# The last 64 queries of two head pairs as one attention unit on all 128 rows

## The chip, the cores and the metric

The kernel runs on one core of a Trainium2 chip. The metric is the device time of one execution in microseconds (us); a kernel's time is the median of its runs. TensorE (PE) multiplies, VectorE (DVE), ScalarE (ACT) and GpSimd (POOL) work on vectors, and SyncE (SP) issues most transfers (DMA). Each engine takes its instructions in the order in which they stand in its own queue, and waits in place if one isn't ready.

## The reference

Attention over a window of 128 positions with a bias that falls with the distance, and then a feed-forward layer with a GELU written with a sigmoid:

```python
# q, k, v: (B=8, H=8, S=576, D=64)
scores = 1/sqrt(D) * q @ k.T                 # per batch and head
scores = where(0 <= rel < 128, scores - slope[h] * abs(rel), -1e9)   # rel = query - key position
attn = exp(scores - max(scores)); attn = attn / (sum(attn) + 1e-9)
x = (attn @ v) as (B*S = 4608 tokens, H*D = 512)
h = x @ w_in                                 # 512 -> 2048
out = (h / (1 + exp(-1.702 * h))) @ w_out    # 2048 -> 512
```

Everything is float32 in and out.

## The kernel before

**Attention units.** Attention is cut into units, each a class instance that later steps hang their tiles on. For batches 2 to 7 a unit is made by `whole_batch`, and the change doesn't touch it. For batches 0 and 1 (`WB = 2`) a batch is cut into three ranges of queries, 0 to 256, 256 to 512 and 512 to 576, and `part_batch` makes one `WholeUnit` for each of the four head pairs (`hp`) in each range. So a batch has 12 units: four with 256 queries, four more with 256, and four with the last 64, called tail units here. A `WholeUnit` holds both heads of its pair (`hh` 0 and 1): q and k lie with the 64 features of head 0 on partitions 0 to 63 and those of head 1 on 64 to 127. Its queries are cut into blocks of up to 128 rows; a tail unit has one block of 64 rows, with 192 keys (the 128 before the range and its own 64).

The steps of such a unit, with the tiles that the profile names:

- `load_whole`, `load_whole_v`: q into `rq`, k into `rk`, v into `VV`.
- `scores`: a float32 product for each block and head, head 0 into `s_ps` and head 1 into `sb_ps` (two PSUM tiles; outside the first four units `sb_ps` is one of the two buffers of `t_ps`).
- `biased` (DVE): scores plus the bias table, into `pb`, and the row's extreme into `mins`.
- `exponents` (ACT): the exponential of `pb`, its sums into `totals`.
- `normal`: DVE makes `rec`, the reciprocals of the sums; POOL scales head 0's block, ACT head 1's.
- `flip_whole`: PE transposes the weights, 128 keys at a time, into `t_ps`; ACT (head 0) and DVE (head 1) copy them to `pw`.
- `mix_whole`: PE multiplies `VV` with `pw` into `x_ps`, head 0 into partitions 0 to 63, head 1 into 64 to 127; ACT copies the result into `xf`, the feed-forward's input.

**Ticks.** A tick advances the units as a pipeline: in tick n unit n is scored and its v is loaded, unit n-1 goes through `biased`, `exponents` and `normal`, unit n-2 is flipped, unit n-3 is mixed, and q and k of unit n+4 are loaded. So the number of units is the number of ticks. Seven ticks run before the feed-forward begins.

**Feed-forward.** Chunks of 256 tokens (`T`), 16 steps (`f`) each: `up` is 12 products into `h_ps`, then a tanh and a product on ACT and DVE (`g`, `gh`), a remainder on POOL (`gl`); `down` is 6 products into `acc`. The first steps go with `decode`, which unpacks a weight block (`rw` into `wc`, `bits`, `w`) on ACT, DVE and POOL, 32 times; its `bits` sits in one of the two PSUM buffers of `h_ps`. The first chunk's first 8 steps come first, then chunk 1, then chunk 0's other 8, then chunks 2 to 11. The last six chunks are taken in pairs by another scheme (`accs`, `X_ps`, `Y_ps`).

**What sets the order.** `advance` places ticks between the steps. For each range it holds a due entry: so many units by the step at which a chunk begins, and it spreads the ticks that are left evenly over the steps that are left. In the program thus written each engine's queue is then put in order by a list scheduler when the kernel is built, apart from transfers that `move` keeps in the order of the program.

## Time and profile before

| | |
|---|---|
| runs | 1047.8, 1050.3, 1045.43 us (median 1047.8) |
| the profiled execution | 1047.39 us, of which the span of instructions is 1045.6 us |
| granted TensorE clock | 0.996 of full speed over the span |
| PE busy | 1027.1 us (98%) |
| ACT, DVE, POOL busy | 675.8, 651.1, 621.2 us (65%, 62%, 59%) |
| DMA | 151.91 MB, mean 145 GB/s |

A row of the timeline gives the start, the length, the engine, the line, the operation with the tiles, the form and how many instructions; in brackets stands the idle time ahead and what ended it. `64*64 64x192` means that a part of the PE array with 64 rows and 64 columns was used, with 192 columns streamed from 64 partitions. A float32 product shows as two instructions, a transposition as one. PE's instructions overlap, so what one costs is the distance from its start to the next start, and not its length.

### The profile page before, as it was taken

Reading aid. Unit: us, or ns where it says so; the run is one execution under the profiler, and the core shown is the slowest. Engines: PE = TensorE matmul, PEld = TensorE weight load, DVE = VectorE, ACT = ScalarE, POOL = GpSimd, SP = SyncE. Lnnn points to the kernel's source line nnn. Section 1 sums busy time; section 2 is a strip of 40 time slices with the busy share of each in tenths; the row PEclk is TensorE's granted clock in tenths of the full one; section 3 lists DMA queues with packets and bytes.
Section 4 is the critical chain, followed back from the end, with each engine's and each line's share of the span. In section 5 each row is a group of like instructions: output and inputs, shape, how many; then the busy total and the mean of one; then the engine's idle time right before and its main releaser. Section 6 shows DMA issues by size and latency. Waiting matters only on the chain.

```text
span 1045.6 us, 21874 instructions
## 1 busy us (share of the span) xinstructions
PE 1027.1 (98%) x6897; PEld 906.8 (87%) x6897; DVE 651.1 (62%) x2250; ACT 675.8 (65%) x1978; POOL 621.2 (59%) x858
## 2 busy tenths in 40 slices
PE   8899999999999999999999999999999999999998
PEld 5577778789999999999999999999898998998997
DVE  6786756367777677777777676766743445346343
ACT  6888855478787777877777786877633334335332
POOL 3687866568677677768667686766542224224221
PEclk9899999999999999999999999999999999999999
DMA  8995445423333233334323433432175556456551
GB/s 290 365 354 167 152 134 159 130 77 100 97 110 100 77 90 121 108 100 129 95 80 102 130 108 90 128 104 68 57 276 181 174 172 219 162 181 207 179 180 61
DMA packets 120275, 151.91 MB, mean 145 GB/s; under 512 B 40032, under 2 KB 96864, under 8 KB 120160
## 3 DMA queue, kind: packets, MB, share of 16 engines
q1 hardware_dynamic: 114400, 140.55, 43.2%
q10 hardware_dynamic: 5760, 9.96, 2.7%
q8 instruction: 55, 0.90, 0.4%
q14 instruction: 60, 0.49, 0.1%
HBM read 119.01 MB, written 31.46 MB: 144 GB/s over the span
## 4 chain that ended last, share of the span: by engine, by line
PE 89%; DMA 4%; DVE 3%; ACT 2%; issue 1%; POOL 1%; SPq 0%; POOLq 0%; ACTq 0%; DVEq 0%
PE h_ps L579 24%; PE acc L599 24%; PE accs L779 12%; PE X_ps L720 6%; PE s_ps L352 5%; PE x_ps L518 5%; PE Y_ps L720 4%; PE t_ps L461 4%; PE x_ps L495 2%; PE t_ps L438 1%; PE sb_ps L342 1%; DMA x<-xf 1%; PE s_ps L342 1%; DMA VV<-v 1%; DMA rk<-k 1%
## 5 line engine op out<-in xcount | busy, mean ns | idle before, releaser
L579 PE MATMUL h_ps<-xh,w 128*128 128x256 f32 x1536 | 245.7, 285 | 2.3 <-DVE g L585 1.4
L579 PEld LDWEIGHTS h_ps<-xh,w 128*128 128x128 f32 x1536 | 212.5, 189 | 18.5 <-DVE g L585 3.3
L599 PE MATMUL acc<-w,gh 128*128 128x512 f32 x768 | 216.3, 399 | 0.8 <-ACT half L616 0.4
L589 POOL TENSOR_TENSOR gl<-g,gh 128x256 fp32r<-128x256 f32 x192 | 144.7, 755 | 100.1 <-ACT gh L588 79.9
L732 POOL TENSOR_TENSOR gs<-g,gs 128x512 fp32r<-128x512 f32 x48 | 63.4, 1320 | 169.9 <-PE Y_ps L720 120.5
L599 PEld LDWEIGHTS acc<-w,gh 128*128 128x128 f32 x768 | 131.2, 188 | 21.3 <-ACT half L616 1.2
L779 PE MATMUL accs<-w,gs 128*128 128x512 f32 x576 | 148.3, 393 | 0.3 <-POOL gs L732 0.3
L579 PE MATMUL h_ps<-xl,w 128*128 128x256 f32 x768 | 138.2, 283 | 0.0
L330 POOL TENSOR_TENSOR K<-rk,K 128x384 fp32r<-128x384 f32 (+1 forms) x120 | 108.6, 905 | 43.0 <-ACT K L328 34.7
L599 PE MATMUL acc<-w,gl 128*128 128x512 f32 x384 | 125.7, 405 | 0.0
L585 DVE SCALAR_TENSOR_TENSOR g<-g,h_ps 128x256 f32<-128x256 f32 x192 | 80.0, 417 | 65.0 <-ACT g L584 62.9
L584 ACT ACTIVATE g<-h_ps 128x256 f32<-128x256 f32 x192 | 72.9, 381 | 70.4 <-PE h_ps L579 61.0
L779 PEld LDWEIGHTS accs<-w,gs 128*128 128x128 f32 x576 | 102.3, 189 | 17.6 <-POOL gs L732 0.7
L579 PEld LDWEIGHTS h_ps<-xl,w 128*128 128x128 f32 x768 | 112.0, 189 | 5.8 <-issue 1.5
L399 ACT ACTIVATE pb<-pb,mins 128x256 f32<-128x256 f32 (+2 forms) x216 | 104.7, 486 | 9.1 <-DVE mins L380 8.6
L588 ACT CAST gh<-g 128x256 fp32r<-128x256 f32 x192 | 77.6, 405 | 41.7 <-DVE g L585 33.4
L380 DVE CUSTOM_DVE_ANT_0 pb<-s_ps,bias 128x256 f32<-128x256 f32 (+3 forms) x240 | 86.1, 380 | 26.5 <-PE s_ps L352 23.4
L424 DVE TENSOR_SCALAR_CACHE_REDUCE pb<-pb,rec 128x256 f32<-128x256 f32 (+2 forms) x216 | 91.1, 454 | 2.9
L329 POOL TENSOR_TENSOR Q<-rq,Q 64x256 fp32r<-64x256 f32 (+1 forms) x120 | 81.8, 682 | 11.7 <-ACT Q L310 2.3
L480 DVE TENSOR_TENSOR pl<-t_ps,ph 128x512 fp32r<-128x512 f32 (+2 forms) x120 | 72.9, 607 | 16.7 <-ACT ph L474 15.6
L461 PE MATMUL t_ps<-ident,pb 128*128 128x128 f32 x408 | 76.7, 272 | 0.0
L352 PE MATMUL s_ps<-K,Q 128*128 128x256 f32 (+1 forms) x432 | 75.8, 288 | 0.0
(114 smaller groups left out, 2000.9 us busy)
## 6 DMA issues: line engine op xcount, KB each, us to landing
ring<-part SPq DMA_DIRECT2D x84, 512.0 KB, 3.3
rk<-kT SPq DMA_DIRECT2D x72, 192.0 KB, 2.8
rq<-qT SPq DMA_DIRECT2D x96, 128.0 KB, 2.6
out<-o ACTq DMA_DIRECT2D x34, 256.0 KB, 2.9
rw<-w_in SPq DMA_DIRECT2D x16, 512.0 KB, 6.7
rw<-w_out SPq DMA_DIRECT2D x16, 512.0 KB, 7.2
x<-xf SPq DMA_DIRECT2D x13, 512.0 KB, 3.5
xf<-x SPq DMA_DIRECT2D x13, 512.0 KB, 4.3
```

The source lines that it names most:

```text
L329: nc.gpsimd.tensor_tensor(Q[D:], rq[D:], Q[D:].bitcast(F32), ALU.subtract)
L330: nc.gpsimd.tensor_tensor(K2, rk, K1.bitcast(F32), ALU.subtract)
L352: nc.tensor.matmul(u.s[:b.rows, e, b.first:b.end], u.Q[:, b.q0 - u.q0:b.q0 - u.q0 + b.rows], k[:, ko:ko + b.end - b.first], start=(z == 0) ...
L380: nc.vector.tensor_tensor_reduce(b.p[ra:rb, cs:b.end], u.s[ra:rb, e, cs:b.end], bias[head][ra:rb, cs:b.end], -SCALE, BIG, ALU.add, ALU.min ...
L399: nc.scalar.activation(live, live, AF.Exp, bias=u.mins[:b.rows, e:e + 1], scale=-1.0, accum_out=u.sums[:b.rows, e, :1],)
L424: nc.vector.tensor_scalar(live, live, u.rec[:rows, e:e + 1], None, ALU.mult, ALU.add, u.rec[:rows, 2 + e:3 + e])
L461: nc.tensor.transpose(u.t[:c.n, w:w + b.rows], b.p[:b.rows, col:col + c.n], ident[:b.rows, :b.rows])
L579: nc.tensor.matmul(h, w1[f][:, z, k * P:(k + 1) * P], x[:, k], start=(n == 0), stop=(n == len(ops) - 1))
L589: nc.gpsimd.tensor_tensor(gl, g, gh.bitcast(F32), ALU.subtract)
L599: products.append(nc.tensor.matmul(acc, g[:, t * P:(t + 1) * P], w2[f][:, z], start=(f == self.f0 and n == 0), stop=(f == self.f1 - 1 and ...
L720: nc.tensor.matmul(bank, w[:, z, k * P:(k + 1) * P], x[:, y, k], start=start and i == 0, stop=i == len(ops) - 1, skip_group_check=True)
L779: products.append(nc.tensor.matmul(self.acc[t], g[:, y, t * P:(t + 1) * P], w2[f][:, z], start=(f == 0 and n == 0), stop=(f == NF - 1 and ...
```

## The change

For batches 0 and 1 the four tail units of a batch become two. A `TailUnit` holds two neighbouring head pairs (`pairs = 2`): the 64 queries of the first pair stand on rows 0 to 63 and those of the second on rows 64 to 127 of the same tiles. q and k of both come with one transfer each, into tiles viewed as `[partition, pair, n]`; v takes one transfer for both pairs' first 128 keys and one for each pair's last 64, of which the second lands in a tile of its own (`rv`). There are four score products as before, each on a quarter of the array, and four calls on DVE (64 rows each), since the bias differs by head. The exponentials, the reciprocals, the scaling, the transpositions and the copies are done once for both pairs on 128 rows. The mixing takes eight products of 64 columns, and one copy brings both pairs into `xf`.

```diff
+class TailUnit(WholeUnit):
+    pairs = 2
+
 def part_batch(b, lo, hi):
+    if hi - lo == HALF:
+        return [TailUnit(b, hp, lo, hi) for hp in range(0, NP, 2)]
     return [WholeUnit(b, hp, lo, hi) for hp in range(NP)]
...
+        if u.pairs == 2:
+            both = slice(u.pair, u.pair + 2)
+            u.rq = u.rq[:, :P].rearrange("p (a n) -> p a n", a=2)
+            u.rk = u.rk.rearrange("p (a n) -> p a n", a=2)
+            move(u.rq, q0[both, :, u.lo:u.hi].rearrange("a p n -> p a n"))
+            move(u.rk, k0[both, :, u.k0:u.hi].rearrange("a p n -> p a n"))
+            return
...
+        if u.pairs == 2:
+            last = raw.tile([P, 3, D], F32, name="rv", bufs=2)
+            u.ends = u.rv[:HALF, 2], last[:HALF, :2]
+            move(u.rv[:, :2], v0[u.pair:u.pair + 2, u.k0:end].rearrange("a p h d -> p a h d"))
+            for a in range(2):
+                move(u.ends[a], v0[u.pair + a, end:u.hi])
+            return
...
+            if u.pairs == 2:
+                for a in range(2):
+                    for hh in range(2):
+                        r = slice(hh * D, (hh + 1) * D)
+                        products.append(nc.tensor.matmul(
+                            u.s[hh][a * HALF:(a + 1) * HALF, 0, :P + HALF], u.rq[r, a], u.rk[r, a],
+                            start=True, stop=True))
+                in_turn(products)
+                return
...
+            if u.pairs == 2:
+                for hh in range(2):
...
+                    for a in range(2):
+                        r, n = slice(a * HALF, (a + 1) * HALF), P + HALF
+                        nc.vector.tensor_tensor_reduce(
+                            p[r, :n], u.s[hh][r, 0, :n], bias[2 * (u.hp + a) + hh][r, a * HALF:a * HALF + n],
+                            -SCALE, BIG, ALU.add, ALU.min, u.mins[r, hh:hh + 1],
+                        )
+                    u.p.append((p, p[:, :n], hh))
+                return
...
-            rows, ne = u.blocks[0][1], len(u.p)
+            rows, ne = u.blocks[0][1] * u.pairs, len(u.p)
...
-                    p, rows = u.p[2 * i + hh][0], u.blocks[i][1]
+                    p, rows = u.p[2 * i + hh][0], u.blocks[i][1] * u.pairs
...
+                if u.pairs == 2:
+                    for k in range(2):
+                        ks = slice(k * HALF, (k + 1) * HALF)
+                        products.append(nc.tensor.matmul(
+                            x[hh * D:(hh + 1) * D, ks], u.ends[k][:, hh] if c else u.rv[:, k, hh], p[:, ks],
+                            start=c == 0 and k == 0, stop=c == 1, skip_group_check=True,
+                        ))
+                    continue
...
+        if u.pairs == 2:
+            ct, o = divmod(u.b * S + u.lo, T)
+            nc.scalar.copy(
+                home(ct)[:, u.hp:u.hp + 2, o:o + n], x[:, :2 * n].rearrange("p (a n) -> p a n", a=2))
+            return
```

There are now 92 units instead of 96, and so four ticks fewer. In batch 0 the tail units were units 8 to 11 and are now 8 and 9; in batch 1 they were 20 to 23 and are now 18 and 19. By the pacing rule the ticks 7 to 10 stand at steps 1 to 4 in both kernels; ticks 11, 12, 13, 14 and 15 move from steps 7, 10, 13, 16 and 19 to steps 8, 12, 16, 20 and 24; from step 65 on the two kernels' ticks coincide, four numbers apart.

On PE, at the end of step 0 of the feed-forward, the order was this (`s_ps` and `sb_ps` with 64x192 are tail units' scores, first of unit 8 and then of unit 9; `t_ps` are transpositions of the units ahead of them; `h_ps` is step 1):

```order
L342 MATMUL s_ps<-rk,rq 64x192
L438 MATMUL t_ps<-ident,pb 128x128 x8
L342 MATMUL sb_ps<-rk,rq 64x192
L438 MATMUL t_ps<-ident,pb 128x128 x4
L342 MATMUL s_ps<-rk,rq 64x192
L438 MATMUL t_ps<-ident,pb 128x128 x4
L579 MATMUL h_ps<-xh,w_1_554 128x256 x8
L579 MATMUL h_ps<-xl,w_1_554 128x256 x4
L342 MATMUL sb_ps<-rk,rq 64x192
```

And now, at the same place (line 365 holds the scores of a tail unit, 484 the transpositions):

```order
L365 MATMUL s_ps<-rk,rq 64x192
L484 MATMUL t_ps<-ident,pb 128x128 x8
L365 MATMUL sb_ps<-rk,rq 64x192
L365 MATMUL s_ps<-rk,rq 64x192
L365 MATMUL sb_ps<-rk,rq 64x192
L484 MATMUL t_ps<-ident,pb 128x128 x6
L365 MATMUL s_ps<-rk,rq 64x192
L484 MATMUL t_ps<-ident,pb 128x128 x2
L638 MATMUL h_ps<-xh,w_1_554 128x256 x8
L638 MATMUL h_ps<-xl,w_1_554 128x256 x4
L365 MATMUL sb_ps<-rk,rq 64x192
L365 MATMUL s_ps<-rk,rq 64x192
```

Three of a unit's four score products now stand together behind the first, and unit 9's first one still stands ahead of step 1.

On DVE, in the same stretch, the order was this (`ISA pb,mins` is the bias step on a head's scores, `wc` and `bits` are two steps of the decoding, `COPY pw` frees a transposition's PSUM):

```order
L369 ISA pb,mins<-sb_ps,bias_78 64x192
L369 ISA mins 64x1
L229 SCALAR_TENSOR_TENSOR wc<-wc,bits 128x512
L228 TENSOR_SCALAR bits<-rw_3_288 128x512
L410 TENSOR_REDUCE rec<-totals 64x2
L411 RECIPROCAL rec<-rec 64x2
L369 ISA pb,mins<-s_ps,bias_79 64x192
L369 ISA mins 64x1
L229 SCALAR_TENSOR_TENSOR wc<-wc,bits 128x512
L228 TENSOR_SCALAR bits<-rw_3_290 128x512
L446 COPY pw<-t_ps 128x512
L229 SCALAR_TENSOR_TENSOR wc<-wc,bits 128x512
```

And now, from the same decoding step (`bits<-rw_3_288`) on:

```order
L237 TENSOR_SCALAR bits<-rw_3_288 128x512
L456 TENSOR_REDUCE rec<-totals 128x2
L457 RECIPROCAL rec<-rec 128x2
L238 SCALAR_TENSOR_TENSOR wc<-wc,bits 128x512
L237 TENSOR_SCALAR bits<-rw_3_290 128x512
L492 COPY pw<-t_ps 128x512
L238 SCALAR_TENSOR_TENSOR wc<-wc,bits 128x512
L237 TENSOR_SCALAR bits<-rw_4_347 128x512
L238 SCALAR_TENSOR_TENSOR wc<-wc,bits 128x512
L237 TENSOR_SCALAR bits<-rw_4_349 128x512
L401 ISA pb,mins<-s_ps,bias_81 64x192
L401 ISA mins 64x1
```

Unit 9's first bias step stood between two decoding steps, ahead of three `wc`; now it stands behind them.

On SP's queue of transfers, behind the loads of unit 9, the order was this (tail units 10 and 11, weights 7 and 11 and the v of unit 8):

```order
L166 DMA rq<-q 128x64
L166 DMA rk<-k 128x192
L166 DMA rw_7_545<-w_in 128x512
L166 DMA rw_7_547<-w_out 128x512
L166 DMA rq<-q 128x64
L166 DMA rk<-k 128x192
L166 DMA rw_11_766<-w_in 128x512
L166 DMA rw_11_768<-w_out 128x512
L166 DMA VV<-v 128x128
```

And now, at the same place:

```order
L175 DMA rq<-q 128x256
L175 DMA rk<-k 128x256
L175 DMA rw_7_545<-w_in 128x512
L175 DMA rw_7_547<-w_out 128x512
L175 DMA rq<-q 128x256
L175 DMA rk<-k 128x256
L175 DMA rw_11_766<-w_in 128x512
L175 DMA rw_11_768<-w_out 128x512
L175 DMA VV<-v 128x2x128
```

Units 10 and 11 are now the first two of batch 1, with 256 queries and 256 keys, so that their larger loads take the places of the two tail units' loads.

More of the change, by code (lines that the diff above doesn't have):

```diff
@@ L134 @@
     whole = True
+    pairs = 1
     def __init__(self, b, hp, lo, hi):
@@ L360, in biased @@
             u.p = []
+            if u.pairs == 2:
+                for hh in range(2):
+                    if hh:
+                        p = att.tile([P, 3 * P], F32, name="pb", tag="K1")
+                    else:
+                        p = att.tile([P, 2 * P], F32, name="pb", bufs=5)
+                    for a in range(2):
[6 more added lines that the diff above has]
+                return
             for i, (at, rows) in enumerate(u.blocks):
```

## The prediction

> **What bounds the kernel now.** I read the busy times by stretch first, since the change lies in the first third of the span. The columns are length, then PE, PE's weight loads, DVE, ACT, POOL, the granted clock, the DMA share and GB/s.
>
> ```profile
> 25.00:50.00 25.00, 19.84 (x122) 13.45 (x123) 17.34 (x59) 21.80 (x62) 16.64 (x18) 0.88 1.01 361
> 50.00:75.00 25.00, 25.00 (x174) 18.03 (x174) 19.89 (x61) 22.71 (x69) 20.15 (x21) 0.98 1.02 352
> 75.00:100.00 25.00, 22.99 (x150) 17.51 (x151) 16.14 (x48) 19.51 (x56) 20.21 (x22) 1.00 0.61 202
> 100.00:150.00 50.00, 49.57 (x318) 40.26 (x317) 35.40 (x91) 37.41 (x107) 41.52 (x43) 1.00 0.52 163
> 150.00:200.00 50.00, 50.00 (x318) 38.12 (x317) 24.99 (x69) 25.79 (x82) 27.75 (x30) 1.00 0.44 134
> ```
>
> From 100 us on PE idles less than 1% of the time (0.4 us of the 100 shown), so there a change is worth what it takes from PE. Ahead of that, three things compete: between 25 and 50 us PE idles 5.2 us while the DMA engines are full, from 50 to 75 us it idles not at all, and from 75 to 100 us 2.0 us. ACT is at 87% and 91% in the first two. Batch 0's tail units lie at 39 to 75 us, batch 1's at 160 to 215 us.
>
> Next the timeline of PE where it idles, and the chain that ended last through the same place:
>
> ```profile
> 42.34 0.54 PE L342 MATMUL sb_ps<-rk,rq 64*64 64x192 f32 x2 [1.20 <-ACT pw L446]
> 43.87 0.92 PE L438 MATMUL t_ps<-ident,pb 128*128 128x128 f32 x4 [0.99 <-POOL pb L420]
> 46.62 0.87 PE L342 MATMUL s_ps<-rk,rq 64*64 64x192 f32 x2 [1.83 <-DMA rk<-k]
> ...
> 48.64 2.08 PE L579 MATMUL h_ps<-xh,w 128*128 128x256 f32 x8
> ```
> ```profile
> 37.80 8.68 DMA rk<-k
> 46.48 0.14 issue
> ...
> 47.63 0.35 DVE pb L369
> 47.99 0.61 DVE wc L229
> ```
>
> The k of tail unit 9 is issued at 37.80 us and lands 8.68 us later, at 46.48; PE waits 1.83 us for it, then DVE does that unit's bias step, then a decoding step `wc` queued behind it, which frees the PSUM that step 1's `h_ps` needs at 48.64.
>
> **The change, part by part.** First the prices of PE's pieces, from start to next start, where nothing idles:
>
> ```profile
> 53.02 0.54 PE L342 MATMUL s_ps<-rk,rq 64*64 64x192 f32 x2
> 53.48 0.33 PE L438 MATMUL t_ps<-ident,pb 64*128 64x64 f32 x2
> 53.74 1.20 PE L579 MATMUL h_ps<-xh,w 128*128 128x256 f32 x8
> ...
> 61.15 0.60 PE L495 MATMUL x_ps<-pw,VV 128*64 128x64 f32 x8
> 61.67 1.19 PE L599 MATMUL acc<-w,gh 128*128 128x512 f32 x4
> ```
> ```profile
> 161.06 1.07 PE L579 MATMUL h_ps<-xh,w 128*128 128x256 f32 x8
> 161.97 0.62 PE L599 MATMUL acc<-w,gl 128*128 128x512 f32 x2
> ...
> 170.81 0.37 PE L342 MATMUL s_ps<-rk,rq 64*64 64x192 f32 x1
> 170.81 0.37 PE L342 MATMUL sb_ps<-rk,rq 64*64 64x192 f32 x1
> 171.02 0.32 PE L342 MATMUL s_ps<-rk,rq 64*64 64x192 f32 x1
> 171.03 0.32 PE L342 MATMUL sb_ps<-rk,rq 64*64 64x192 f32 x1
> 171.28 0.62 PE L579 MATMUL h_ps<-xh,w 128*128 128x256 f32 x3
> ...
> 188.26 0.44 PE L438 MATMUL t_ps<-ident,pb 64*128 64x64 f32 x4
> 188.63 0.54 PE L342 MATMUL s_ps<-rk,rq 64*64 64x192 f32 x2
> 189.10 1.19 PE L579 MATMUL h_ps<-xh,w 128*128 128x256 f32 x8
> 190.13 0.62 PE L579 MATMUL h_ps<-xl,w 128*128 128x256 f32 x4
> ```
> ```profile
> 109.09 0.49 PE L438 MATMUL t_ps<-ident,pb 128*128 128x128 f32 x3
> 109.34 0.72 PE L599 MATMUL acc<-w,gl 128*128 128x512 f32 x2
> ```
>
> One tail score alone costs 0.46 us (53.02 to 53.48); both heads' scores side by side cost 0.47 together (170.81 to 171.28), so two quarters of the array work at once. Two tail transpositions cost 0.26, four 0.37. A unit's whole mixing costs 0.52. After a piece that uses only a part of the array, eight `h_ps` products cost 1.03 (189.10 to 190.13) instead of 0.91 (161.06 to 161.97): the change of form costs about 0.12 us behind it, and I take 0.2 for both sides of an excursion from the full array.
>
> *Scores.* Before, 16 products: by the order 7 stand alone (0.66 with the excursion), 7 lie inside longer excursions (about 0.47), one pair is side by side (0.67): 4.6 + 3.3 + 0.7 = 8.6 us. After, again 16, but 4 alone (2.6), three groups of three (`sb_ps`, `s_ps`, `sb_ps`), one pair (0.7) and one inside an excursion (0.5). A group of three uses three different quarters. If all three overlap it costs what the pair costs, 0.67, 0.67 and, in a longer excursion, 0.5: 5.6 us in all, 3.0 saved. If only two can, each costs up to 0.63 more: 7.5 us, 1.1 saved. I take 2.4, nearer to the overlap, since the row at 170.81 shows it whole for two. The Trainium skill ("TensorEngine Tiling (Array Packing)", Key Properties) has different tiles load and multiply independently, four of them in the 64×64 form; by that the saving is 3.0, and no row here shows three or four.
>
> *Transpositions.* 32 of 64 columns become 16 of 128, so what is streamed stays the same. Half of them (128 keys) take the full array, at 0.08 us each (three in 0.25, from 109.09) without an excursion, 0.7 us with 8; the other half (64 keys) take a part of it, and in the new order 6 of these 8 stand alone: about 0.25 (nearly all of which is fixed, as in the 0.26 above) + 0.2 each, the others 0.35, 3.4 us. Before, the 32 stood in 8 pieces of two (0.26) and 4 of four (0.37), 4 of them excursions of their own (0.2): 4.4 us. Saved 0.3; bounds 0.9 saved (all small ones inside other excursions, 0.35 each) and 0.3 lost (0.1 more for each of the six).
>
> *Mixing.* 32 products of 64 columns before and after. Before, 5 units were mixed in one piece (0.52) and 3 in 8 pieces of 0.26: 4.7 us. After, order and price give 10 pieces: four of one product (0.26), two of two (0.3), two of five (0.73), one of six and one of eight (0.84, 0.94): 4.9 us, and about four more excursions of their own, 0.8. Lost 1.0; bounds 0 and 1.3 lost.
>
> *ACT, DVE, POOL.*
>
> ```profile
> L392 ACT ACTIVATE pb<-pb,mins 64x192 f32<-64x192 f32 x16 | 7.3, 458 | 3.3 <-DVE mins L369 3.3
> L420 POOL TENSOR_SCALAR pb<-pb,rec 64x192 f32<-64x192 f32 x8 | 6.5, 813 | 1.7 <-DVE rec L411 1.6
> L417 ACT ACTIVATE pb<-pb,rec 64x192 f32<-64x192 f32 x8 | 3.7, 466 | 0.9 <-DVE rec L411 0.9
> L399 ACT ACTIVATE pb<-pb,mins 128x192 f32<-128x192 f32 x3 | 1.4, 454 | 0.0
> ```
>
> An exponential on 128 rows takes 454 ns, on 64 rows 458: rows cost nothing. So ACT loses 8 exponentials (3.7 us) and 4 scalings (1.9), POOL 4 scalings (3.3), half of each in batch 0. DVE's 16 bias steps stay 16. From 100 us on this is worth nothing: PE covers it. In batch 0 it may count, see the rivals.
>
> *Transfers and order.* The same bytes move, but earlier: units 8 and 9 load both pairs' q and k, 128 KB more each.
>
> ```profile
> DMA packets 12474, 21.26 MB, mean 354 GB/s; under 512 B 1615, under 2 KB 8875, under 8 KB 12465
> ```
>
> At the 354 GB/s of 20 to 80 us, 256 KB are 0.7 us, so unit 9's k lands at about 47.2 instead of 46.48, and PE waits there until then. Against that, unit 9's bias step no longer stands ahead of the three `wc` steps on DVE, so step 1 starts when unit 9's score (0.46) and two transpositions (0.2) are through, at about 47.9 instead of 48.64. Net 0.7 us saved; bounds 1.4 saved (k no later) and 0.7 lost (another wait ends last). Behind unit 9, SP now brings units 10 and 11 with 256 KB of q and k each instead of 128; unit 10's first score stands at 53.02 (above) without a wait, so I cost this at nothing; without that room it is the second rival.
>
> *Ticks.* Tick 11 moves from step 7 to 8 and tick 12 from 10 to 12, so the attention done per step around 75 to 100 us gets less; of the 2.0 us that PE idles there I take 0.6 as saved, between 2.0 saved and 2.0 lost.
>
> Sum: scores -2.4, transpositions -0.3, mixing +1.0, step 1 -0.7, ticks -0.6: -3.0 us. The profiled execution took 1047.4 us (span 1045.6), so 1044.4; the median of the runs lies 0.4 above it: 1044.8. The low ends of the terms add up to -7.3 (-3.0, -0.9, 0, -1.4, -2.0), the high ends to +3.2 (-1.1, +0.3, +1.3, +0.7, +2.0): 1040.5 and 1051.0.
>
> **The rivals.** Within 0.5% (5.2 us) a measurement of this kernel hardly tells anything from no change; its three runs differ by 4.9 us.
>
> *ACT is the bound of batch 0's stretch.* For it: ACT is at 87 and 91% from 25 to 75 us, and PE waits there for `pw` and `pb` (1.20 and 0.99 us). Then batch 0's half of ACT's saving, 2.8 us, comes off too: 1042.0, just faster. Against it: the ticks of steps 1 to 4 stay, and bring larger units.
>
> *The loads arrive late.* Units 10 and 11 take the tail units' places on SP's queue:
>
> ```profile
> 46.14 0.34 SPq L166 DMA_DIRECT2D rq<-q  x1
> 46.53 0.42 SPq L166 DMA_DIRECT2D rk<-k  x1
> ```
>
> If the k issued at 46.53 again takes 8.68 us, as at 37.80, and 384 KB more go with or ahead of it (1.1 us at 354 GB/s), it lands at 56.3, 3.3 us behind the place of unit 10's score (53.02), and PE and the decoding behind DVE's bias step wait; unit 11, next on the queue, loses as much again. Then -3.0 becomes +3.6: 1051.4. It decides once that transfer takes over 5.4 us (53.02 less 46.53 less 1.1). Against it: the score at 53.02 shows no wait for its load now, so the load took less than 6.5 us.
>
> *Nothing is won on PE.* The groups of three don't overlap (1.1 saved), the mixing loses 1.3, and step 1 and the ticks give nothing: 1047.8 - 1.1 - 0.3 + 1.3 = 1047.7. For it: by the order, PE leaves the full array 65 times now and 64 times before, so the price of these excursions, which a merging should spare, stays. The Trainium skill (same page and section) has every change of the tiling mode drain TensorE; the 1.03 us at 189.10 against 0.91 at 161.06 agree.
>
> **How the numbers follow.** My forecast (PE saves 1 to 2 us, step 1 and the ticks as much): 0.45, with 1043 to 1047. Nothing won: 0.2. ACT as the bound: 0.25. Late loads: 0.1. The forecast's time is 1044.8. The range goes from the sum's low end, 1040.5, to 1050.5, short of its high end: it leaves out most of the late loads (0.08) and the cases in which ACT's saving comes on top of a sum near its low end (0.08). Faster by over 0.5% means below 1042.6: ACT's case, mostly, and a little of the forecast, 0.27; slower (above 1053.0): a part of the late loads, 0.07; the rest, 0.66, lies within.
>
> **What the profile would show.** The score groups: three 64x192 scores from `sb_ps` to the next start in about 0.5 us (overlap) or 0.8. The transpositions on 128 rows with 64 outputs: 0.25 us alone. Step 1's `h_ps` at about 47.9, with a wait for `rk` of about 2.5 us ahead of unit 9's score. No wait for unit 10's or 11's k. ACT's share in 25 to 75 us below 91%. PE's idle time from 75 to 100 us below 2.0. From 100 us on, no new idle time, and the last tail unit done 2 to 3 us earlier. I am wrong if PE waits for a load between 50 and 75 us, or if the waits of 42 to 47 us vanish altogether, which the order doesn't suggest.

## The result, and the profile after

The changed kernel takes 1040.33 us (median of five runs, 1039.7 to 1040.42); before took 1046.9 in the same comparison (1045.21 to 1050.3). The ratio is 0.9936 with a 95% interval of 0.9924 to 0.9949: 6.6 us faster. The forecast was 1044.8 us with a range from 1040.5, so the time lies 0.2 us below the range, and the gain is over twice the 3.0 us forecast. The profiled execution took 1039.7 us, its span 1037.9. One of the six executions of the experiment e6 below took 2014.33 us; it counts in that run's median of 1041.03 (1040.88 without it) and not in its ratio.

The busy times by stretch, of after, with the columns as before (length; PE, weight loads, DVE, ACT, POOL; granted clock, DMA share, GB/s):

```profile
25.00:50.00 25.00, 20.96 (x132) 14.98 (x132) 19.50 (x64) 23.14 (x63) 17.68 (x18) 0.88 1.03 376
50.00:75.00 25.00, 24.83 (x190) 18.23 (x189) 21.31 (x70) 23.59 (x73) 19.93 (x21) 0.99 1.01 348
75.00:100.00 25.00, 23.83 (x146) 17.90 (x144) 17.29 (x45) 19.97 (x58) 20.18 (x23) 1.00 0.58 200
100.00:150.00 50.00, 47.83 (x312) 39.10 (x310) 34.10 (x80) 34.92 (x94) 39.95 (x42) 1.00 0.50 157
150.00:200.00 50.00, 50.00 (x331) 40.95 (x330) 27.77 (x84) 25.66 (x78) 30.63 (x36) 1.00 0.48 146
```

PE idles 4.0 us instead of 5.2 between 25 and 50 us, and 1.2 instead of 2.0 between 75 and 100, but 0.2 instead of 0.0 between 50 and 75 and 2.2 instead of 0.4 between 100 and 150. Up to the end of chunk 3 its waits of more than 0.15 us add up to 9.6 us before and 9.9 after. So the gain up to there is no shorter wait; it lies in what PE's pieces cost.

Where it appears, the copies of the finished chunks show. Between 80 and 400 us chunks 1, 2, 3 and 4 end with two `o<-acc` each on DVE; a row gives the count, the lengths in ns and the first and the last start. First before, then after:

```profile
L626 DVE TENSOR_SCALAR o<-acc x8: 680/684/692, 155.0 to 375.8; 128x512 f32<-128x512 f32 x8
```
```profile
L685 DVE TENSOR_SCALAR o<-acc x8: 679/683/691, 155.2 to 369.3; 128x512 f32<-128x512 f32 x8
```

The same copies between 200 and 330 us, which are those of chunks 2 and 3:

```profile
L626 DVE TENSOR_SCALAR o<-acc x4: 680/681/692, 250.6 to 314.6; 128x512 f32<-128x512 f32 x4
```
```profile
L685 DVE TENSOR_SCALAR o<-acc x4: 679/682/687, 245.8 to 307.5; 128x512 f32<-128x512 f32 x4
```

At 155 us the feed-forward is no further than before, since until then the gain is spent on attention that is a unit ahead (76 instructions into `s_ps` instead of 72). By the end of chunk 2 (251.9 us before, 247.1 after) 4.8 us are won, by the end of chunk 3 (315.3 and 308.2) 7.1, and at the end of chunk 4 the distance is 6.5.

Batch 0's waits, by PE's timeline of after:

```profile
41.91 0.37 PE L365 MATMUL sb_ps<-rk,rq 64*64 64x192 f32 x1 [0.78 <-ACT pw L492]
...
44.68 1.54 PE L484 MATMUL t_ps<-ident,pb 128*128 128x128 f32 x6 [2.22 <-POOL pb L466]
46.15 0.90 PE L365 MATMUL s_ps<-rk,rq 64*64 64x192 f32 x2
...
47.32 2.06 PE L638 MATMUL h_ps<-xh,w 128*128 128x256 f32 x8
```

The wait for the `rk` of unit 9 (1.83 us before) is gone, and the wait for POOL's scaled `pb` is 2.22 us instead of 0.99: PE comes to the same place and waits for another. Step 1 starts at 47.32 instead of 48.64. That the wait for `rk` is gone holds for this execution only: e14 and e18 (below) run the same program up to here, and in their traces PE waits 0.75 and 0.89 us for it.

Last, tail scores of batch 1, three at a time in three quarters of the array:

```profile
162.24 0.52 PE L365 MATMUL sb_ps<-rk,rq 64*64 64x192 f32 x2
162.45 0.32 PE L365 MATMUL s_ps<-rk,rq 64*64 64x192 f32 x1
162.45 0.32 PE L365 MATMUL sb_ps<-rk,rq 64*64 64x192 f32 x1
162.71 0.33 PE L484 MATMUL t_ps<-ident,pb 128*128 128x128 f32 x1
```

The first row joins an instruction of each of two `sb_ps` products, the others are second instructions; with the first `s_ps` at 162.23 three scores are through 0.48 us after they began, where one score alone cost 0.46.

### The profile page after: what moved, and what is told of

It is laid out like the page before. It is cut to its first block, busy times and chain, and to the rows that moved or that the text cites. A ratio compares the mean times of both kernels' runs of the same rounds, so it can differ in the third digit from the quotient of the medians.

```text
span 1037.9 us, 21750 instructions
## 1 busy us (share of the span) xinstructions
PE 1020.1 (98%) x6881; PEld 905.4 (87%) x6881; DVE 651.2 (63%) x2234; ACT 668.8 (64%) x1946; POOL 616.6 (59%) x854
## 4 chain that ended last, share of the span: by engine, by line
PE 89%; DVE 3%; DMA 3%; ACT 2%; issue 1%; POOL 1%; SPq 0%; POOLq 0%; ACTq 0%; DVEq 0%
PE h_ps L638 24%; PE acc L658 24%; PE accs L838 12%; PE X_ps L779 6%; PE s_ps L384 5%; PE x_ps L577 5%; PE Y_ps L779 4%; PE t_ps L507 4%; PE x_ps L549 1%; PE t_ps L484 1%; DMA rw<-w_in 1%; PE s_ps L374 1%; PE sb_ps L374 1%; DMA VV<-v 1%; ACT pb L438 1%
## 5 line engine op out<-in xcount | busy, mean ns | idle before, releaser
L638 PE MATMUL h_ps<-xh,w 128*128 128x256 f32 x1536 | 242.9, 285 | 1.8 <-DVE g L644 1.5
```

Of the source, the lines that this page charges most:

```text
L638: nc.tensor.matmul(h, w1[f][:, z, k * P:(k + 1) * P], x[:, k], start=(n == 0), stop=(n == len(ops) - 1))
```

## Where the time went, piece by piece

Summed from start to next start over all of PE's products up to the end of chunk 3 (waits over 0.15 us taken out), PE's work falls from 304.1 to 296.8 us:

| pieces | before | after | difference | forecast |
|---|---|---|---|---|
| tail scores | 7.40 | 4.91 | -2.5 | -2.4 |
| transpositions, all | 23.27 | 22.40 | -0.9 | -0.3 |
| tail mixing | 4.96 | 4.47 | -0.5 | +1.0 |
| `h_ps` and `acc` (the same products) | 199.2 | 195.4 | -3.8 | not in the sum |
| other attention, empty products | 69.2 | 69.5 | +0.3 | not in the sum |

The comparison with the forecast is rough in each row, since the forecast's terms hold the whole price of an excursion, and a part of that falls on the product behind and so into the fourth row.

Two things that the forecast didn't count go through these rows.

*Changes of form.* Going through PE's products in order of start and counting each place where the form (`64*64`, `128*64`, ...) differs from the one ahead, up to 330 us, gives 178 changes before and 145 after. Of the 33 saved, about 10 lie in each of the stretches to 150 and from 150 to 200 us, 13 behind 200 us. The excursions from the full array are 64 and 65. Their number stays since the feed-forward is interrupted as often; but before, the pieces of tail units and their neighbours stood in several partial forms one behind the other. The prediction's rows at 188.26, 188.63 and 189.10 are such a place: `x_ps` in 128\*64, `t_ps` in 64\*128, `s_ps` in 64\*64, `h_ps` in 128\*128 is one excursion with four changes. What stands ahead of them in the timeline of before:

```profile
187.23 0.74 PE L599 MATMUL acc<-w,gl 128*128 128x512 f32 x2
187.90 0.43 PE L495 MATMUL x_ps<-pw,VV 128*64 128x128 f32 x2
```

The transpositions carried two partial forms then, and carry one now (groups of before, then of after: busy us, mean ns, idle us):

```profile
L438 PE MATMUL t_ps<-ident,pb 64*128 64x64 f32 x16 | 3.7, 256 | 0.0
L438 PE MATMUL t_ps<-ident,pb 64*64 64x64 f32 x16 | 3.1, 216 | 0.0
```
```profile
L484 PE MATMUL t_ps<-ident,pb 128*64 128x128 f32 x8 | 2.1, 272 | 0.0
```

*A float32 piece in the full form.* The feed-forward's operands have the type `F32R` in the code (`xh`, `xl`, `gh`, `gl`), the transpositions and batch 0's and 1's scores and mixing plain `F32`. In both kernels a feed-forward product that stands directly behind a transposition costs 0.087 us more than one behind its like, although the form stays 128\*128; outside the throttled stretch this happens 55 times before and 42 times after. That is 1.1 us of the 3.8; products beside a partial form account for 1.3 more, and the rest isn't tied to a neighbour (I take it for stalls below the 0.15 us). That the type makes those 0.087 us isn't shown apart from what else differs between the pieces.

Both were readings of one pair of traces, so e14, e15, e18 and e19 measure them by themselves.

## The experiments

Each is compared with before on the same chip in the same comparison; "gain" is the difference of the medians. "Changes" is the count of changes of form up to 330 us in the experiment's own trace (before 178, after 145).

**One batch at a time.** In `part_batch`:

```diff
-    if hi - lo == HALF:
+    if hi - lo == HALF and b == 0:      # e1; b == 1 in e2
```

> The change for batch 0 alone (batch 1 keeps four tail units of 64 rows). Theory P: the gain is PE's own work on the tail units (scores of three quarters at once, half the transpositions), the same in both batches; then this keeps about half of the 6.6 us: 1043.6 us, between 1042.5 and 1044.7. Rival W: the gain is in the waits and the load on ACT, POOL and DVE while the weights are decoded, which only batch 0's tail units meet; then nearly all of it is here: 1040.3 to 1041.5.

Measured: 1041.31 us (before 1047.38), ratio 0.9946 [0.9933, 0.9958], gain 6.1; 153 changes.

> The change for batch 1 alone. Theory P: about half of the gain, 1043.6 us, between 1042.5 and 1044.7. Rival W: nothing, 1046 to 1047.

Measured: 1043.35 us, ratio 0.9963 [0.9949, 0.9977], gain 4.0; 161 changes. Both halves of the change win, and together they would make 10, where the whole makes 6.6 to 7.0. By the expectations' numbers, batch 0 alone fits the rival (nearly all of the gain there) and batch 1 alone the theory (half of it), so this pair decides for neither. The changes of form don't add up either: 25 and 17 fewer, but 33 for both. What is left of each gain beside 0.114 us for each change (below) is 3.2, 2.1 and 2.8 us; that these don't add up isn't explained.

**The number of ticks.** After, with an empty tick behind each tail unit, so that there are 96 again; and before, with the tail's ticks run in pairs, so that it has the pacing of after:

```diff
-        return [TailUnit(b, hp, lo, hi) for hp in range(0, NP, 2)]
+        return [u for hp in range(0, NP, 2) for u in (TailUnit(b, hp, lo, hi), None)]   # e4
```
```diff
+PAIRED = 9, 11, 21, 23      # e7, on the kernel before; a pair counts once in the pace
...
             tick()
+            if ticks in PAIRED:
+                tick()
```

> The changed kernel with an empty tick behind each merged unit, so that there are 96 ticks at the steps of the kernel before. Theory P: PE's work is the same, 1040.3 to 1041.3. Rival T: the gain comes from four ticks fewer, which leave other ticks and loads in better places; then half of it or more goes: 1043.5 to 1047.

Measured: 1040.4 us (before 1047.38), ratio 0.9936 [0.9923, 0.9948]; 144 changes.

> The kernel before, with its units of 64 rows, but with two tail units' ticks run together as one for the pacing, so that the ticks and the loads fall at the steps of the changed kernel. Theory P (work saved on the engines): no gain, 1046.5 to 1048. Rival T (pacing): half of the gain or more, 1040.5 to 1044.

Measured: 1045.17 us (before 1046.52), ratio 0.9989 [0.9980, 0.9998], gain 1.3 with an interval from 0.2 to 2.1; 170 changes, 8 fewer than before, whose price would be 0.9. With the ticks of before the changed kernel keeps its whole gain (e4), with the ticks of after the kernel before gains at most a third of it. So pacing isn't where the gain comes from; whether it is worth the 0.6 us of the forecast's term, these runs don't show.

**ACT and POOL.** The merged unit's exponentials and scalings are done on 64 rows again, as two instructions, with PE's part left merged: in both batches (e3), in batch 0 (e8), in batch 1 (e9), in batch 0 for ACT alone (e10) and for POOL alone (e11). The diff is that of e8; e3 has no condition on the batch, e9 has `u.b == 1`, e10 and e11 keep one of the two engines' instructions whole:

```diff
+            if u.pairs == 2 and u.b == 0:
+                for _, live, e in u.p:
+                    for a in range(2):
+                        r = slice(a * HALF, (a + 1) * HALF)
+                        nc.scalar.activation(live[r], live[r], AF.Exp, ...)
+                return
...
+                        if engines[e] == "A":
+                            nc.scalar.activation(live[r], live[r], AF.Copy, scale=u.rec[r, e:e + 1])
+                        else:
+                            nc.gpsimd.tensor_scalar(live[r], live[r], u.rec[r, e:e + 1], None, ALU.mult)
```

> The changed kernel, but the exponentials and the scalings of a tail unit are done for 64 rows at a time, so that ACT and POOL get back the 8 exponentials (3.7 us with 458 ns each), 4 scalings each (1.9 and 3.3 us) that the change took from them; PE's work is that of the changed kernel. Theory P: within 1 us of the changed kernel, 1040.3 to 1041.3. Rival W (ACT is the bound of batch 0's stretch): 2.8 us more, 1043.

Measured: 1044.74 us (before 1047.38), ratio 0.9978 [0.9969, 0.9987]: a gain of 2.6, so some 4 us of the whole change's gain are gone, more than the theory (at most 1) and the rival (2.8) expected. It isn't the changes of form: 148, against 145 after.

> The changed kernel with the exponentials and scalings of 64 rows at a time in batch 0 alone: ACT gets back 4 exponentials and 2 scalings (2.8 us), POOL 2 scalings. Theory W (ACT is the bound of batch 0's stretch, 25 to 75 us, and of that alone): all of the 4.4 us that the split cost in both batches, 1044 to 1045. Rival: the split costs wherever it stands, since PE waits for these steps in its own order; then half, 1042.5.

Measured: 1042.89 us (before 1046.52), ratio 0.9969 [0.9958, 0.9980], gain 3.6: some 3 us gone, again with 145 changes.

> The same split in batch 1 alone, where PE hardly idles. Theory W: nothing, 1040 to 1041. Rival: half of the 4.4 us, 1042.5.

Measured: 1040.59 us (before 1046.52), ratio 0.9946 [0.9934, 0.9958], gain 5.9: at most 1 us gone.

> The changed kernel with ACT's exponentials and scalings of batch 0's two merged units done for 64 rows at a time (4 exponentials and 2 scalings more, 2.8 us by the rows of before); POOL scales 128 rows at once as in the changed kernel. Theory W, ACT: nearly all of the 3.4 us that the split of both cost in batch 0, a ratio to the kernel before of 0.996 to 0.997. Rival, POOL: the ratio of the changed kernel, 0.9936, or 0.5 us more.

Measured: 1041.03 us (before 1046.96), ratio 0.9945 [0.9932, 0.9958], gain 5.9: 0.7 us less than after, which its interval doesn't tell from nothing.

> The counterpart: only POOL's scaling of batch 0's merged units is done for 64 rows at a time (2 more, 1.6 us). Theory W, ACT: the changed kernel's ratio, 0.9936 to 0.9945. Rival, POOL: 0.996 to 0.997.

Measured: 1040.07 us (before 1046.96), ratio 0.9939 [0.9924, 0.9954], gain 6.9: nothing gone. And the other way about, after with ACT relieved: for units 4 to 9 DVE scales head 1's blocks.

```diff
-            engines = "PPVA" if u.early else "PAPA"
+            engines = "PPVA" if u.early else "PVPV" if u.at < 10 else "PAPA"
```

> The changed kernel with head 1's scaling of the units 4 to 9 (batch 0, outside the first four) moved from ACT to DVE: ACT loses 10 scalings of about 0.5 us in 25 to 65 us, DVE gains them. Theory W, ACT is the bound there: 2 to 4 us faster than the changed kernel, a ratio of 0.990 to 0.992. Rival: DVE takes ACT's place, 0.993 to 0.998.

Measured: 1041.15 us (before 1046.96), ratio 0.9943 [0.9929, 0.9956], gain 5.8: nothing more comes off, although ACT is busy 19.08 us instead of 23.14 from 25 to 50 us. But DVE took that work, 22.22 us instead of 19.50, so that, as the expectation's rival has it, DVE may have taken ACT's place.

So 64 or 128 rows don't matter in batch 1, as forecast. In batch 0, ACT is full in e10 between 60 and 75 us and not in after (first after, then e10; ACT is the fourth engine).

```profile
60.00:75.00 15.00, 15.00 (x116) 11.20 (x116) 11.62 (x39) 13.59 (x44) 12.16 (x14) 1.00 1.03 358
```
```profile
60.00:75.00 15.00, 15.00 (x124) 11.64 (x123) 12.54 (x38) 15.00 (x48) 13.38 (x15) 1.00 1.01 334
```

Chunk 0's first half ends at 92.5 us in e10 and 90.5 in after, but by the end of chunk 0 both stand at 187.3 to 187.4. Half of these 2 us is there ahead of that stretch, from a transfer: in e10 PE waits for unit 9's k, which lands at 47.04 us instead of 45.53, and comes to that unit's first score at 47.17 instead of 46.15.

```profile
47.17 0.87 PE L365 MATMUL s_ps<-rk,rq 64*64 64x192 f32 x2 [1.57 <-DMA rk<-k]
```

That the full ACT makes the other half is possible and not shown. Then e10 makes up for the delay; it has 130 changes of form, 15 fewer than after, which at 0.114 us would be 1.7, but no run takes that apart. The rival "ACT is the bound" is thus not shown in either direction: with more ACT work no loss can be told, and with less nothing comes off, though there DVE stands in the way.

**The order and the shape of PE's pieces.** In e6 the mixing goes by pair and then by head, where after goes by head and then by pair:

```diff
-            for hh in range(2):
-                p = u.pt[hh][c]
-                if u.pairs == 2:
-                    for k in range(2):
+            if u.pairs == 2:
+                for k in range(2):
+                    for hh in range(2):
```

> The changed kernel with the mixing's products in another order: the two heads of a pair one behind the other (they use two halves of the array), then the next pair, where the changed kernel has both pairs of one head first. If the mixing is worth what its starts show (4.5 us for 64 instructions, 0.07 each), pairing the heads saves at most 0.8 us: 1039.5 to 1040.5. If the order of the list scheduler matters more than PE's work, it lies 1 us or more to either side.

Measured: 1041.03 us (before 1046.52), ratio 0.9942 [0.9929, 0.9955]; 145 changes: no difference from after that can be told. In e12 the second transposition takes all 128 keys up to the end (the last 64 of them are used, on partitions 64 to 127), so that it has the full form:

```diff
+                    if u.pairs == 2:
+                        n, col = P, min(col, HALF)
...
-            u.ends = u.rv[:HALF, 2], last[:HALF, :2]
+            u.ends = u.rv[HALF:, 2], last[HALF:, :2]
```

> The changed kernel with the second transposition of a merged unit's head over 128 keys (the last 64 of them are used, on partitions 64 to 127, where v's end is loaded too), so that PE keeps the full array for all 16 transpositions and one copy replaces two. Theory P (a change of the array's form costs 0.1 to 0.25 us): 8 lone pieces of 0.25 + 0.2 us become 8 of about 0.1, less what stood inside other excursions: 1 to 2.5 us faster than the changed kernel, 1038 to 1039.5, a ratio of 0.991 to 0.9927. Rival: the forms cost nothing that other work doesn't cover, 0.993 to 0.9945.

Measured: 1039.55 us (before 1046.96), ratio 0.9929 [0.9916, 0.9942]; 132 changes. It is the lowest median of all (gain 7.4), but its interval overlaps that of after. Thirteen changes fewer would be 1.5 us; 0.8 were measured (against after in its own comparison), so this run neither bears out the price of a change nor contradicts it.

**The price of a piece and of a change.** After, with one extra product of 64 columns ahead of each of the 96 `h_ps` groups of chunks 4 to 9, in the form 64\*64 (e14) or 128\*128 (e15):

```diff
+            if self.c in EXTRA:      # range(4, 10); chained ahead of the group's products
+                first.append(nc.tensor.matmul(
+                    h[:HALF, :HALF], ident[:HALF, :HALF], ident[:HALF, :HALF], start=True, stop=True))   # e14
+                    h[:, :HALF], ident[:, :], ident[:, :HALF], start=True, stop=True))                   # e15
```

> The changed kernel with 96 extra 64x64 products of 64 columns, one ahead of each h_ps group of chunks 4 to 9 (overwritten by it, so no part of the result). By the order 47 of them stand between two full-array pieces, 45 have one full-array and one partial neighbour. Theory 'the change of form costs' (the prediction's prices: 0.13 us for the product, 0.2 for an excursion, 0.1 for half of one): 96 x 0.13 + 47 x 0.2 + 45 x 0.1 = 26 us over the changed kernel, about 1066. Rival 'a lone piece costs its own stream and nothing behind it': 96 x 0.13 = 12 us, about 1053, and as much as the full-array variant sent with it within 5 us.

Measured: 1084.78 us (before 1046.29), ratio 1.0371 [1.0357, 1.0385]. That is 44.5 us above after, 0.46 for each piece. That is far above the 26 us of its theory. One reason is that attention beside chunks 4 to 9 uses the full form throughout, so all 96 are excursions (the trace has 337 changes against 145, 192 more); the other is the price of the product itself, which e15 shows.

> The same 96 extra products at the same places, of 64 columns too, but 128x128, so PE stays in the form of its neighbours. Theory 'the change of form costs': 96 x 0.05 to 0.08 = 5 to 8 us over the changed kernel, 1045 to 1048, some 18 less than the partial variant. Rival 'a lone piece costs the same in any form': within 5 us of the partial variant.

Measured: 1062.46 us, ratio 1.0155 [1.0141, 1.0169]: 22.1 us above after, 0.23 for each piece, where 5 to 8 us, 0.05 to 0.08 each, were expected. The rival "costs the same in any form" falls: the two differ by 22.3 us, which is 0.23 for an excursion and 0.116 for each of its two changes. The timelines of e14 and then e15 show where it lies:

```profile
403.88 0.62 PE L642 MATMUL h_ps<-xl,w 128*128 128x256 f32 x4
404.42 0.33 PE L640 MATMUL h_ps<-ident 64*64 64x64 f32 x2
404.68 1.21 PE L664 MATMUL acc<-w,gh 128*128 128x512 f32 x4
405.73 0.28 PE L642 MATMUL h_ps<-xh,w 128*128 128x256 f32 x1
```
```profile
398.45 0.62 PE L642 MATMUL h_ps<-xl,w 128*128 128x256 f32 x4
398.90 1.09 PE L664 MATMUL acc<-w,gh 128*128 128x512 f32 x4
399.82 0.33 PE L640 MATMUL h_ps<-ident 128*128 128x64 f32 x2
399.96 0.71 PE L664 MATMUL acc<-w,gl 128*128 128x512 f32 x2
400.51 1.08 PE L642 MATMUL h_ps<-xh,w 128*128 128x256 f32 x8
```

The full piece takes 0.14 and the two products behind it 0.55 (0.46 or 0.47 elsewhere). The partial one takes 0.26, the four products ahead of it 0.54 instead of 0.45, and the four behind it 1.05 instead of 0.92: 0.48 in all.

Then three extra products at each of these places, twice 64\*64 (a) and once 128\*64 (b), in the sequence a, a, b (e18) or a, b, a (e19). The same products and the same 140 excursions more than after, but 359 changes more against 428:

```diff
+                first.append(nc.tensor.matmul(h[:HALF, 0*HALF:1*HALF], ident[:HALF, :HALF], ident[:HALF, :HALF], ...))   # a
+                first.append(nc.tensor.matmul(h[:HALF, 1*HALF:2*HALF], ident[:HALF, :HALF], ident[:HALF, :HALF], ...))   # a; b in e19
+                first.append(nc.tensor.matmul(h[:HALF, 2*HALF:3*HALF], ident[:, :HALF], ident[:, :HALF], ...))           # b; a in e19
```

> Three extra products of 64 columns ahead of each of the 96 h_ps groups of chunks 4 to 9 (overwritten by them): two 64x64 (a), then one 128x64 (b). By the order, some groups are drawn apart: 140 excursions from the full array in all, and 359 changes of form. Theory 'every change of form costs', also between two partial forms: 0.115 us each (half of the 0.23 by which a lone partial product cost more than a lone full one). Rival 'only leaving and re-entering the full array costs': the same excursions, so the same time as the other sequence, within 2 us. Both: the changed kernel + 288 x 0.23 (the product alone, by the full-array run) + 140 x 0.23 = about 98 us, 1138.

Measured: 1131.28 us (before 1047.07), ratio 1.0806 [1.0791, 1.0821]: 91 us above after, where 98 were expected.

> The same products in the sequence a, b, a: again 140 excursions, but 428 changes of form, 69 more. Theory 'every change of form costs': 69 x 0.115 = 8 us longer than the sequence a, a, b. Rival 'only leaving and re-entering the full array costs': within 2 us of it.

Measured: 1139.17 us, ratio 1.0881 [1.0866, 1.0895]. The traces have 504 and 573 changes and 205 excursions each. So 69 changes between partial forms cost 7.9 us, 0.114 each (0.112 by the fastest execution of either, 1130.82 and 1138.57 us): as much as a change from or to the full array. The rival, that only leaving the full array costs, falls. The same group in e18 and in e19:

```profile
405.67 0.32 PE L640 MATMUL h_ps<-ident 64*64 64x64 f32 x2
405.84 0.28 PE L641 MATMUL h_ps<-ident 64*64 64x64 f32 x2
406.04 0.33 PE L642 MATMUL h_ps<-ident 128*64 128x64 f32 x2
406.30 0.38 PE L644 MATMUL h_ps<-xh,w 128*128 128x256 f32 x1
```
```profile
405.77 0.33 PE L640 MATMUL h_ps<-ident 64*64 64x64 f32 x2
406.02 0.33 PE L641 MATMUL h_ps<-ident 128*64 128x64 f32 x2
406.28 0.33 PE L642 MATMUL h_ps<-ident 64*64 64x64 f32 x2
406.54 0.39 PE L644 MATMUL h_ps<-xh,w 128*128 128x256 f32 x1
```

A product with its like behind it takes 0.17, one with another form behind it 0.20 to 0.26; the group takes 0.63 in one sequence and 0.77 in the other. The Trainium skill ("TensorEngine Tiling (Array Packing)", Key Properties) has each change of the tiling mode drain TensorE, with no price; these runs agree and give one, 0.114 us.

**The clock.** Why does splitting both engines' work in batch 0 (e8) cost 3 us, when either alone costs nothing that can be told? The traces of e3 and e8 show a lower granted clock already from 10 to 15 us, 0.70 and 0.74, where after's shows 1.00 (the 0.93 in the expectation of e16 is e8's mean over the first 25 us). So the split kernel and the changed kernel were run with 9 instead of 11 empty products at the start:

```diff
-FIRST_SPINS = 11
+FIRST_SPINS = 9
```

> The kernel that splits ACT's and POOL's tail work of batch 0 into 64 rows (3.4 us lost), with 9 instead of 11 empty products before the first score, so that the first 75 us meet the clock at another phase. Theory 'the clock': its loss comes from the granted clock of 0.93 from 10 to 15 us and again from 45 to 60; where that falls away, it comes within 1.5 us of its partner (the changed kernel with the same 9). Rival 'load': ACT and POOL together are what is late in batch 0, so it stays 2.5 to 3.4 us behind its partner whatever clock the profile shows. If the clock of 10 to 15 us is as low as before, this run tells nothing new.

Measured: 1042.33 us (before 1046.29), ratio 0.9964 [0.9952, 0.9977].

> The changed kernel with 9 instead of 11 empty products before the first score: partner of the split kernel with 9. Both theories: 1039.5 to 1041 if its clock in the first 25 us stays at 1.00; the theory 'the clock' 1041 to 1042.5 if it falls to about 0.93 there, the rival 'load' no change even then.

Measured: 1039.74 us, ratio 0.9939 [0.9927, 0.9952]. The difference of 2.6 us stays, and so does the clock. From 10 to 15 and from 50 to 60 us, e16 and then e17 (the third number from the end is the clock):

```profile
10.00:15.00 5.00, 4.94 (x27) 3.04 (x29) 2.88 (x18) 4.37 (x19) 1.82 (x3) 0.66 0.99 372
...
50.00:60.00 10.00, 9.71 (x66) 7.02 (x64) 8.65 (x27) 9.85 (x27) 6.18 (x7) 0.87 1.02 343
```
```profile
10.00:15.00 5.00, 4.37 (x35) 2.84 (x36) 3.38 (x19) 4.37 (x18) 2.03 (x4) 1.00 1.01 382
...
50.00:60.00 10.00, 8.89 (x66) 6.47 (x63) 9.66 (x33) 10.00 (x31) 7.39 (x8) 1.00 1.02 349
```

Both stretches are throttled in the one kernel and neither in the other, though the two programs differ only from batch 0's tail on. By its own expectation this pair tells nothing new. Another trace does: e18, which splits nothing and is after's program up to chunk 4, has the same low clock, so the split isn't needed for it. Its row, and then the first score of unit 8 in e8 and in e18:

```profile
10.00:15.00 5.00, 4.34 (x25) 2.81 (x27) 3.47 (x21) 4.34 (x18) 2.42 (x4) 0.74 1.02 397
```
```profile
40.55 0.54 PE L365 MATMUL s_ps<-rk,rq 64*64 64x192 f32 x2
```
```profile
40.56 0.54 PE L366 MATMUL s_ps<-rk,rq 64*64 64x192 f32 x2
```

After's stands at 39.57. So in these traces 1.0 us is lost ahead of the first instruction that the split touches, and in e18 it is still 1.0 at the end of chunk 1 (`o<-acc` from 156.19 us, after's from 155.18), where e8 is 2.9 behind (158.09). Against e19, which is the same program up to chunk 4 and had the full clock, e18 is 1.7 behind there (154.48). The low clock thus accounts for 1 to 1.7 of the 2.9 us in e8's profiled execution; what makes the rest, and whether the other executions had that clock, stays open. It doesn't touch the comparison of before and after: there the clock is 0.88 and 0.88 from 25 to 50 us, 0.98 and 0.99 from 50 to 75.

## Why the prediction was wrong

Two steps of the sum failed, both on what PE's pieces cost. The mixing was put at +1.0 us and measured -0.5, and the `h_ps` and `acc` products, which the sum left at nothing, cost 3.8 us less. In the other direction, shorter waits (step 1 and ticks) were to bring 1.3 us, and up to the end of chunk 3 the waits grew by 0.3. With the table's -7.3 that gives 7.0 us, about the 7.1 by which chunk 3 ends earlier.

*Scores* (-2.4 forecast, -2.5 measured): right, and right for its reason. Three quarters of the array work at once, 0.48 us for three scores. The Trainium skill ("TensorEngine Tiling (Array Packing)", Key Properties), which the prediction cited, has different tiles load and multiply independently; this trace agrees for three.

*Transpositions* (-0.3; -0.9) and *mixing* (+1.0; -0.5): both mis-sized, the transpositions at their low bound, the mixing with the wrong sign and outside its bounds of 0 to +1.3. Both were priced by excursions from the full array, with "about four more excursions of their own, 0.8" for the mixing. The price was good (0.2 taken, 0.23 measured), but the sum doesn't fit its own count. It charges one excursion less for the scores, two more for the transpositions and four more for the mixing, five more in all (1.0 us), where its count, like the traces, has one more (64 and 65): 0.8 us too much. The unit of account was wrong too. Each change of form costs, and those within an excursion went from 178 less 2 x 64, that is 50, to 15. At 0.114 us the 33 saved would make 3.8 us, spread over the rows of the table above, over half of the gain. This is an estimate from the price that e18 and e19 gave for extra products; no experiment takes the changes alone out of the tail, and e1, e2, e10 and e12 don't follow the count closely.

*The products around.* The sum took the `h_ps` and `acc` products as unchanged, since they are the same instructions. They cost 3.8 us less, 1.3 of it beside partial forms (a part of the same 33 changes, told above) and 1.1 because fewer of them stand behind a float32 transposition.

*Step 1 earlier* (-0.7; 1.3 at that place): the start came at 47.32, not 47.9. The expected wait of 2.5 us for `rk` didn't come: the text held it for an error if the waits of 42 to 47 us vanish, "which the order doesn't suggest"; one vanished and POOL's grew. The k of unit 9 was issued at 36.99 us instead of 37.80, and it was there when PE came at 46.15; in other executions of the same program it came later (e18: issued at 37.84, landed at 47.27), so this part was luck. By 155 us nothing of it is left in the feed-forward's progress.

*Ticks* (-0.6): neither shown nor refuted. e4 loses nothing with the ticks of before, e7 gains 0.2 to 2.1 us with those of after.

*The rivals.* Late loads: didn't come; between 50 and 75 us PE waits for no load. Nothing won on PE: its argument (65 excursions against 64, so the price stays) is the same error of account, in the open. ACT as the bound: in its form (2.8 us more come off because ACT is relieved) not shown. The split in batch 0 does take 3 us, but with ACT's alone no loss can be told, and moving more of ACT's work to DVE gives nothing; and ACT's share from 50 to 75 us rose to 94% where below 91% was forecast, while larger units had moved in.

*The other signs.* PE's idle time from 75 to 100 us fell to 1.2 (forecast: below 2.0). From 100 to 150 us there is new idle time, 2.2 us against 0.4, where none was forecast; that is about as much as the stretches 25 to 50 and 75 to 100 had won (1.2 and 0.8). The last tail unit was to be done 2 to 3 us earlier; its copy into `xf` starts at 205.34 us instead of 215.53, 10 us earlier.

## What to carry to other kernels

Where TensorE is the bound, count the changes of the array's form along its queue, between two partial forms too, and not only the departures from the full array; here each cost 0.114 us, and at that price over half of what merging the small units won lies in the changes that it spared. A small piece between large products also has a price when it keeps the full form: 0.23 us for a float32 product of 64 columns, of which 0.14 is its own and 0.09 falls on the product behind it. So a sum over the instructions that an edit touches can miss half its worth (3.8 of 7.3 us here), since the instructions beside them change their cost. And a wait of a microsecond for a transfer that shows in one execution can be absent in the next: compare it over several traces of the same program before a term rests on it.

## What the runs showed of the hardware

- A change between two partial forms costs 0.114 us (e18 and e19), a change from or to the full form 0.116 (e14 and e15): it makes no difference which.
- A feed-forward product directly behind a float32 piece in the same 128\*128 form costs 0.087 us more (42 to 55 such places in each kernel, and 67 of e15's pieces up to 600 us).
- The granted clock fell at 10 to 15 us to between 0.66 and 0.74 in four traces (e3, e8, e16, e18) and stayed at 1.00 in the others; these programs differ from after's or e17's only behind 39 us, e18's only from chunk 4 on. No run shows why.
- The k of unit 9 took 8.5 to 10.1 us from issue to landing in traces of the changed kernel and its variants, and PE waited between nothing and 1.57 us for it.
